# Attention with a routed expert layer on one core: ten head pairs instead of eight have two query tiles turned by DMA, and the first expert weights load five steps later

## The chip, the core and the metric

The kernel runs on one core of a Trainium2 chip. Its engines are PE (TensorE: matmuls and transposes; PEld are its weight loads), DVE (VectorE), ACT (ScalarE), POOL (GpSimd) and SP (SyncE, which here only issues DMAs). The metric is the device time of one execution in microseconds (us), lower is better. A verdict compares the medians of kernels that were timed on the same chip.

## The reference

Attention for 4 batches, 8 heads, 576 positions and 64 features per head, with a bias that a two-layer net computes from the relative position, and behind it an expert layer in which each token goes through one of 8 experts (512 to 1024 to 512). The output is the expert layer's.

```python
scores = scale * np.matmul(q, k.transpose(0, 1, 3, 2))
...
scores = scores + bias.transpose(2, 0, 1)[None, :, :, :]
scores = scores - np.max(scores, axis=-1, keepdims=True)
attn = np.exp(scores)
attn = attn / (np.sum(attn, axis=-1, keepdims=True) + 1e-09)
return np.matmul(attn, v).astype(np.float32)
...
fresh_e = int(np.argmax(logits[b, s]))
if s == 0 or local_gate[b, s] < 0.5:
    e = fresh_e
else:
    e = prev_e if prev_e >= 0 else fresh_e
...
h = np.maximum(x[b, s] @ w1[e], 0.0)
out[b, s] = p[e] * (h @ w2[e])
```

Here x is the attention's output, logits and local_gate are two small products of it, and p is the softmax of the logits.

## The kernel before

**Pairs and units.** Heads are worked in pairs (p, b): p is 0 to 3 (heads 2p and 2p+1), b the batch. The 16 pairs come in the order of the list `pairs`: p = 0 and p = 1 for all four batches, then (2,0), (2,1), (3,0), (3,1), (2,2), (2,3), (3,2), (3,3). From the fifth pair on each pair is nine units: four query tiles of 128 rows with two heads each, and one tile that holds the last 64 rows of both heads. `emit_s` makes a unit's scores: four f16 matmuls into a PSUM tile `sps` (lines 305, 306; 316 for the last tile), of which there are two buffers, then DVE adds the bias and finds the extreme (line 325), then ACT takes the exponential with its row sum (line 330).

**Turning e.** The second product needs the exponentials e with keys on the partitions. There are two ways.

- By TensorE (`emit_t`, `emit_av`): per unit four f32 transposes into PSUM tile `ta` (line 396), an ACT copy to SBUF tile `eT` (lines 400, 402), per query tile one more transpose into `tb` (line 412) with a DVE copy (line 413), then f32 matmuls with v (lines 422, 426).
- By DMA, for pairs in the list `DMP` and there only for the first two query tiles of the order: ACT casts e to an f16 high part (line 336), DVE subtracts it from e for an f16 low part (`emit_lo`, line 346), SP issues one transposing DMA per query tile (line 350), and `av_split` makes three f16 products from high and low parts (lines 363, 369). The high and low parts of v for such a pair are made two pairs ahead by DVE (line 276) and POOL (line 119). Such a pair's output rows are cast on ACT instead of POOL (line 480), and their store to HBM is issued five units later (`LST`).

**Order of the work.** Calls are collected in a list `ev` with a key in units (`at(u + offset, ...)`) and run in the order of the keys. A Tile scheduler then orders each engine's instructions, except for SP between the units S1 and S2, where SP keeps the order in which the calls stand. Every engine works its own instructions in order.

**Routing beside attention.** When batches 0 and 1 are done, `route_first` runs one step per unit: it finds the first two blocks of 128 tokens that share an expert (matmuls into the same `sps` buffers, two scans and many small operations on DVE), then loads block 0's first-layer weights (`load_w(0, 0)`, 2 MB into the tiles `ws`), and some units later splits them into f16 high and bf16 low parts (`split_ops`: ACT cast line 910, DVE or POOL subtraction lines 917, 119). `fetch_first` gathers the tokens of these two blocks and loads block 0's second-layer weights into `wb`. The table `early` places further splits in the last eight units. A load whose expert is that of the block before is conditional (`cond`) and moves nothing then.

**Memory.** The f16 parts of e and v lie in pools (`dmx`) that `open_w` closes; the weight tiles `ws` and `we` are opened in their place. At unit SL the staging tiles of q and k (`stgx`) are closed and a second-layer weight tile is opened.

**After attention** the routing of all tokens runs beside the layers of blocks 0 and 1, and then the other blocks follow.

Of the kernel before, what the change touches and what calls it, by code (L numbers as in the profile page):

```python
# [17 lines left out]
B, H, S, D = 4, 8, 576, 64  # L18
# [31 lines left out]
def build(tc, nc, io):  # L50
# [202 lines left out]
    groups = [(0, b, qt) for g in (QORD[0:2], QORD[2:]) for bb in ((0, 1), (2, 3)) for qt in g for b in bb]  # L253
    pairs = [(p, b) for p in range(NP - 2) for b in range(B)]
# [3 lines left out]
    units = []  # L258
# [2 lines left out]
            units.append((gi, x))  # L261
    e_t, eT_t, hs_t = {}, {}, {}
    e16_t, v16_t, av_t = {}, {}, {}
    DMP = pairs[B:B + 8]
    dmx = ExitStack()
    dbox = {}
    pend, ucur = [], [0]
# [2 lines left out]
    def prefetch(gi):  # L270
        p, b, qt = groups[gi]
        if (p, b) in DMP and qt == QORD[0]:
            if "e" not in dbox:
# [19 lines left out]
    def emit_s(u):  # L293
# [36 lines left out]
        nc.scalar.activation(out=e, in_=e, func=AF.Exp, scale=-1.0, bias=st[:, 0:1], accum_out=sm)  # L330
        if (p, b) in DMP and qt in QORD[0:2]:
            if hh == 0:
# [21 lines left out]
    def av_split(p, b, part=None):  # L354
# [19 lines left out]
            return  # L374
        eT_t.pop((p, b, 0))
        v16_t.pop((p, b))
        xt = xt_t[p, b] = xt_p.tile([128, SP], F32, name="xt")
        if p >= NP - 2:
            nc.vector.memset(xt[:, S:SP], 0.0)
# [2 lines left out]
    def emit_t(u):  # L382
        gi, hh = units[u]
        p, b, qt = groups[gi]
        g = grp(qt)
        if (p, b) in DMP and g == 0:
            return
# [61 lines left out]
    def emit_rows(p, b, u):  # L449
# [29 lines left out]
        on_act = p == 0 or (p == NP - 1 and b >= 2)  # L479
        (nc.scalar.copy if on_act or (p, b) in DMP else cast_pool)(out=hi, in_=xr)  # L480
        (sub_dve if on_act and (p, b) != (NP - 1, B - 2) else sub_pool)(lo, xr, hi)
# [90 lines left out]
    def open_w():  # L572
        dmx.close()
        ws = ctx.enter_context(tc.tile_pool(name="ws0", bufs=1, side="right"))
        for c in range(2):
            stage_t[0].append(ws.tile([128, 2048], F32, name=f"ws0{c}"))
        rbox["w"] = ctx.enter_context(tc.tile_pool(name="we", bufs=1, side="right"))
# [62 lines left out]
    NU = len(units)  # L640
    ex_t = {}

    def emit_out(p, b, gi):
        emit_rows(p, b, gi + 1)
        if (p, b) == DMP[-1]:
            open_w()

    def emit_gates(p, b):
        if p >= NP - 2:
# [106 lines left out]
    def route_first():  # L756
# [78 lines left out]
            in1=tv.unsqueeze(3).to_broadcast([128, NQ, b1, K1]), op=ALU.mult,  # L835
        )
        one_hots(ng, RHA1, RHP1)
        yield
        load_w(0, 0)
        yield  # L840
        ps = s_ps.tile([128, 2, 512], F32, name="sps")
# [3 lines left out]
        nc.vector.tensor_scalar(out=ex, in0=ex, scalar1=-1.0, scalar2=1.0, op0=ALU.mult, op1=ALU.add)  # L845
        nc.vector.tensor_tensor(out=R["tokb"][:, :, 0:b1], in0=ex, in1=tv, op=ALU.mult)
        yield
        for _ in range(3):
            yield
        for f in split_ops(0, 0, on_pool=((1, 1),)):  # L850
            f()
# [228 lines left out]
    for u in range(NU):  # L1080
        gi, hh = units[u]
        p, b, qt = groups[gi]
# [25 lines left out]
    ev.sort(key=lambda e: e[0:2])  # L1108
    ev = [e for e in ev if e[0] < NU]

    S1, S2 = [min(u for u in range(NU) if groups[units[u][0]][0:2] == pairs[i]) for i in (B + 0, B + 9)]
    SL = 1 + min(u for u in range(NU) if groups[units[u][0]][0:2] == pairs[-3])

    def run(a, b):
        for key, _, f in ev:
# [409 lines left out]
```

## Time and profile before

| What | Value |
|---|---|
| median of 3 runs | 581.9 us (580.81 to 582.47) |
| the profiled execution | 579.53 us, of which its span is 577.7 us |
| PE busy | 530.2 us (92%) |
| DVE busy | 468.2 us (81%) |
| ACT busy | 436.6 us (76%) |
| POOL busy | 260.4 us (45%) |
| mean granted TensorE clock | 0.979 of full speed |

The span is the time from the first to the last instruction; 1.83 us of the profiled execution lie around it. Busy shares are means over stages that differ: the bias tables and p = 0 come up to about 130 us, the other pairs up to about 340 us, and then the expert blocks to the end. Matmuls are pipelined and their ends are modelled, so a PE that is shown busy isn't PE at its peak; where a price of PE is wanted, it is better taken from the starts of instructions that follow each other.

### The profile page before, as it was taken

What the parts mean: (1) busy time and instruction counts of PE and PEld (TensorE: products, weight loads), DVE (VectorE), ACT (ScalarE), POOL (GpSimd) and SP (SyncE); (2) the same over time, 40 slices, a digit from 0 to 9 for tenths busy, and PEclk for the clock granted to TensorE, in tenths of its full rate; (3) what the DMA queues carried; (4) which work ended last, traced back from release to release, by engine and by line L of the source; (5) the groups of instructions that cost most, each with busy time, mean ns of one, the idle gap of its engine ahead of it and who ended that gap; (6) DMA issues with size and microseconds to landing.
All of it is one profiled execution on the core that took longest, in us unless ns stands there. A gap on an engine that the chain in (4) does not pass through costs nothing. (4 is left out here: it accounts for less than half of the span.)

```text
span 577.7 us, 14240 instructions
## 1 busy us (share of the span) xinstructions
PE 530.2 (92%) x5302; PEld 359.0 (62%) x5319; DVE 468.2 (81%) x914; ACT 436.6 (76%) x742; POOL 260.4 (45%) x293
## 2 busy tenths in 40 slices
PE   5679999989978999999899999999999999999991
PEld 1124445756755667767586676577686867777851
DVE  6888885688888989797888468779999799898950
ACT  5879877867978887877589865468998787986840
POOL 5200000795299969858547560622433354334111
PEclk9799999999999999999999998799999999999997
DMA  8766546756798799646084012866999947878240
GB/s 278 258 175 186 143 133 194 262 161 154 193 240 226 204 255 247 188 105 190 23 289 117 2 42 71 218 220 218 290 260 293 332 146 191 161 214 225 36 180 30
DMA packets 99613, 106.15 MB, mean 184 GB/s; under 512 B 66893, under 2 KB 76239, under 8 KB 95442
## 3 DMA queue, kind: packets, MB, share of 16 engines
q1 hardware_dynamic: 94752, 89.45, 55.0%
q0 software_dynamic: 4640, 15.43, 9.1%
q8 instruction: 44, 0.72, 0.5%
q10 hardware_dynamic: 146, 0.30, 0.2%
q14 instruction: 31, 0.25, 0.1%
HBM read 128.92 MB, written 20.80 MB: 259 GB/s over the span
## 5 line engine op out<-in xcount | busy, mean ns | idle before, releaser
L330 ACT ACTIVATE e<-e,st 128x576 f32<-128x576 f32 x144 | 111.5, 776 | 16.5 <-DVE st L325 13.1
L325 DVE CUSTOM_DVE_ANT_0 e<-sps,wb 128x576 f32<-128x576 f32 x144 | 107.0, 749 | 18.1 <-PE sps L306 13.3
L917 DVE TENSOR_TENSOR w<-wb,w 128x2048 bf16<-128x2048 f32 (+1 forms) x36 | 72.3, 2050 | 1.9 <-ACT w L910 1.6
L402 ACT COPY eT<-ta 128x512 f32<-128x512 f32 x96 | 55.0, 582 | 21.8 <-PE ta L396 14.6
L305 PE MATMUL sps<-kh,qs 128*128 128x288 f16 x256 | 68.3, 288 | 3.4 <-DVE st L325 2.8
L1014 POOL DMA_INDIRECT out_dram<-y,odx x17 | 30.3, 1781 | 90.2 <-ACT y L1004 58.9
L396 PE MATMUL ta<-c_cpb,e 128*128 128x128 f32 x448 | 70.1, 277 | 0.2
L306 PE MATMUL sps<-kl,qs 128*128 128x288 f16 x256 | 68.0, 286 | 0.0
L910 ACT CAST w<-wb 128x2048 f16<-128x2048 f32 (+1 forms) x40 | 63.8, 1641 | 2.6 <-DMA wb<-in_w_dram 2.6
L988 PE MATMUL yp<-w,hhT 128*128 128x512 f16 (+1 forms) x255 | 64.3, 384 | 1.5 <-ACT w L910 0.5
L211 PE MATMUL sps<-hd,c_cpa 128*32 128x512 f32 (+17 forms) x352 | 49.2, 517 | 15.0 <-DVE hd L197 10.6
L949 PEld LDWEIGHTS <-we 128*128 128x128 f16 (+1 forms) x1056 | 59.9, 98 | 2.4
L949 PE MATMUL sps<-xT,we 128*128 128x128 f16 (+1 forms) x1056 | 61.1, 219 | 0.0
L426 PE MATMUL av<-eT,vt 128*64 128x320 f32 (+1 forms) x384 | 60.8, 424 | 0.0
L396 PEld LDWEIGHTS ta<-c_cpb,e 128*128 128x128 f32 x448 | 52.0, 141 | 10.0 <-issue 2.2
L197 DVE TENSOR_SCALAR hd<-tab,bp 128x448 f32<-128x448 f32 (+17 forms) x130 | 50.1, 445 | 3.6 <-PE sps L211 3.6
L949 PE MATMUL sps<-xT,wb 128*128 128x128 f16 (+3 forms) x1056 | 50.1, 209 | 0.7 <-issue 0.7
L949 PEld LDWEIGHTS <-wb 128*128 128x128 f16 (+1 forms) x1056 | 48.1, 99 | 3.8 <-issue 2.5
L917 DVE TENSOR_TENSOR we<-ws,we 128x2048 bf16<-128x2048 f32 (+1 forms) x25 | 48.9, 1995 | 1.1 <-ACT we L910 1.1
L988 PEld LDWEIGHTS <-hhT 128*128 128x128 f16 x272 | 26.2, 100 | 30.3 <-issue 3.0
L426 PEld LDWEIGHTS av<-eT,vt 128*64 128x64 f32 x384 | 26.2, 136 | 26.6 <-issue 10.4
L910 ACT CAST we<-ws 128x2048 f16<-128x2048 f32 (+1 forms) x26 | 41.2, 1636 | 0.0
(234 smaller groups left out, 1013.2 us busy)
## 6 DMA issues: line engine op xcount, KB each, us to landing
ws<-in_w_dram SPq DMA_DIRECT2D x34, 1024.0 KB
wb<-in_w_dram SPq DMA_DIRECT2D x34, 1024.0 KB
hs<-in_w_dram SPq DMA_DIRECT2D x20, 1024.0 KB
bias_d<-bv SPq DMA_DIRECT2D x36, 295.5 KB
kf<-in_kt_dram SPq DMA_DIRECT2D x24, 288.0 KB
wb<-bias_d SPq DMA_DIRECT2D x16, 288.0 KB
wb<-bias_d SPq DMA_DIRECT2D x16, 256.0 KB
xrow_d<-xo SPq DMA_DIRECT2D x16, 256.0 KB
```

What stands on the lines that cost most here:

```text
L197: nc.vector.tensor_scalar(out=hd[:, 0:n], in0=tab[:, 0:n], scalar1=bp[:, k:k + 1], scalar2=0.0, op0=ALU.add, op1=ALU.max,)
L305: nc.tensor.matmul(out=ps[:, half, 0:288], lhsT=lq, rhs=kh[:, j], start=True, stop=False)
L306: nc.tensor.matmul(out=ps[:, half, 0:288], lhsT=lq, rhs=kl[:, j], start=False, stop=True)
L325: nc.vector.tensor_tensor_reduce(out=e, in0=ps[:, :, 0:288], in1=bsl, scale=-0.125, scalar=1e30, op0=ALU.add, op1=ALU.min, accum_out=st[:, ...
L330: nc.scalar.activation(out=e, in_=e, func=AF.Exp, scale=-1.0, bias=st[:, 0:1], accum_out=sm)
L396: nc.tensor.transpose(out=ta[:, j, :], in_=e[:, o:o + 128], identity=ident)
L402: nc.scalar.copy(out=eTv[:, :, hh, o:o + 128], in_=ta)
L426: nc.tensor.matmul(out=av[64 * x:64 * x + 64, 0:n], lhsT=vt[:, j, 64 * x:64 * x + 64], rhs=eT[:, 2 * j + x, 0:n], start=False, stop=(j == 3),)
L910: nc.scalar.copy(out=wh[c][:, sl], in_=src)
L917: nc.vector.tensor_tensor(out=wl[c][:, sl], in0=src, in1=wh[c][:, sl], op=ALU.subtract)
L949: nc.tensor.matmul(out=hp.rearrange("p a j -> p (a j)")[:, n * f:n * f + n], lhsT=w[f // 4][:, o:o + 128], rhs=x[:, kt], start=(i == 0), s ...
L988: nc.tensor.matmul(out=yp, lhsT=x[:, kt], rhs=w[kt // 4][:, 512 * (kt % 4):512 * (kt % 4) + 512], start=(i == 0), stop=(i == len(terms) - 1),)
```

## The change

`DMP` takes in two more pairs, (2,2) and (2,3), so ten pairs have their first two query tiles turned by DMA. The pools `dmx` are needed longer by that, so `open_w` moves from the output of the last `DMP` pair into `av_split`, behind the last matmul that reads them. `load_w(0, 0)` comes five steps of `route_first` later, and the four splits of these weights four steps later. Block 1's first-layer load, which stands behind them, thereby comes after the first two of block 1's splits (in `early`), which read the tiles that it would fill; it is conditional on an expert other than block 0's. S2 moves by one pair: SP keeps the written order up to the first unit of (3,2) instead of (2,3). SL moves by 12 units.

```diff
@@ -261,7 +261,7 @@
-    DMP = pairs[B:B + 8]
+    DMP = pairs[B:B + 10]
@@ -374,6 +374,8 @@
             return
         eT_t.pop((p, b, 0))
         v16_t.pop((p, b))
+        if (p, b) == DMP[-1]:
+            open_w()
@@ -642,8 +644,6 @@
     def emit_out(p, b, gi):
         emit_rows(p, b, gi + 1)
-        if (p, b) == DMP[-1]:
-            open_w()
@@ -835,7 +835,8 @@
         one_hots(ng, RHA1, RHP1)
-        yield
+        for _ in range(6):
+            yield
         load_w(0, 0)
@@ -845,7 +846,7 @@
         yield
-        for _ in range(3):
+        for _ in range(2):
             yield
         for f in split_ops(0, 0, on_pool=((1, 1),)):
@@ -1108,8 +1109,8 @@
-    S1, S2 = [min(u for u in range(NU) if groups[units[u][0]][0:2] == pairs[i]) for i in (B + 0, B + 9)]
-    SL = 1 + min(u for u in range(NU) if groups[units[u][0]][0:2] == pairs[-3])
+    S1, S2 = [min(u for u in range(NU) if groups[units[u][0]][0:2] == pairs[i]) for i in (B + 0, B + 10)]
+    SL = 13 + min(u for u in range(NU) if groups[units[u][0]][0:2] == pairs[-3])
```

Lines 377 to 645 of the kernel before stand two lines further down in the changed one (413 becomes 415), those behind line 838 one line.

Three places show how instructions move. The first is DVE in the routing steps of pair (2,3), before (full, thr, gp are small tiles of `route_first`, e16_3451 and c16 its one-hot rows, sps the PSUM tile of scores):

```order
L779 TENSOR_REDUCE full_3901<-nbc_3482 16x1
L780 SCALAR_TENSOR_TENSOR gp_3479<-ca_3899,c_cpb_116 16x2
L325 ISA e_3895,st_3923<-sps_3918,wb0_126 128x576
L325 ISA st_3923 128x1
L785 SCALAR_TENSOR_TENSOR thr_3905<-full_3901,ca_3899 16x1
L413 COPY eT_3928<-tb_r_108 128x128
L788 SCALAR_TENSOR_TENSOR e16_3451<-cs_3481,thr_3905,e16_3451 16x576
L800 COPY cb_3955<-sps_3935 16x2
L791 TENSOR_TENSOR c16_3449<-e16_3451,cs_3481 16x576
L325 ISA e_3943,st_3944<-sps_3938,wb0_126 128x576
L325 ISA st_3944 128x1
L801 SCALAR_TENSOR_TENSOR gp_3479<-cb_3955,c_cpb_116 16x2
```

And with the change, where the two low parts of (2,3) (e16_3846 and e16_3886) stand in the middle of the steps:

```order
L779 TENSOR_REDUCE full_3893<-nbc_3482 16x1
L346 TENSOR_TENSOR e16_3846<-e_3842,e16_3846 128x1152
L785 SCALAR_TENSOR_TENSOR thr_3897<-full_3893,ca_3891 16x1
L325 ISA e_3882,st_3934<-sps_3929,wb0_126 128x576
L325 ISA st_3934 128x1
L788 SCALAR_TENSOR_TENSOR e16_3451<-cs_3481,thr_3897,e16_3451 16x576
L800 COPY cb_3954<-sps_3940 16x2
L791 TENSOR_TENSOR c16_3449<-e16_3451,cs_3481 16x576
L325 ISA e_3948,st_3949<-sps_3943,wb0_126 128x576
L325 ISA st_3949 128x1
L346 TENSOR_TENSOR e16_3886<-e_3882,e16_3886 128x1152
L801 SCALAR_TENSOR_TENSOR gp_3479<-cb_3954,c_cpb_116 16x2
```

Between the same two routing operations (lines 779 and 801) two large subtractions have come in, and the copy of line 413 has gone. The second place is SP's queue from pair (2,3)'s loads to the weights, before:

```order
L145 DMA vt_3828<-in_vl_dram 128x640
L490 DMA xrow_d_60<-xo_3775 128x4x128
L493 DMA xrow_d_60<-xo_3775 64x128
L631 DMA xrow_d_60<-pr_3448 128x4x8
L634 DMA xrow_d_60<-pr_3448 64x8
L878 TENSOR_LOAD emap_405
L878 ISA x2
L884 ISA
L884 DMA ws00_3783<-in_w1_dram 128x2048
```

And with the change:

```order
L145 DMA vt_3817<-in_vl_dram 128x640
L350 DMA_TRANSPOSE eT_3889<-e16_3846 128x18x128
L492 DMA xrow_d_60<-xo_3760 128x4x128
L495 DMA xrow_d_60<-xo_3760 64x128
L350 DMA_TRANSPOSE eT_3889<-e16_3886 128x18x128
L879 TENSOR_LOAD emap_405
L879 ISA x2
```

The two transposing DMAs of (2,3) stand between the loads of q, k and v for (3,3) and the read of the expert's number, and the probabilities' store (line 631) has moved ahead of those loads. The third place is ACT behind the last unit of attention, before (w110 and w101 are second-layer weight parts, wb1 holds block 1's first-layer parts, sums the row sums, tmb the gate logits' addends):

```order
L910 CAST w110_4613<-wb0_126 128x1024
L480 CAST xo_4663<-xr_79 128x5x128
L910 CAST w110_4613<-wb0_126 128x1024
L446 ACTIVATE sums_121<-sums_121 128x5x2
L910 CAST w101_4614<-wb0_126 128x1024
L539 COPY tmb_4708<-lg_120 128x45
```

And with the change:

```order
L911 CAST w110_4619<-wb0_126 128x1024
L482 CAST xo_4669<-xr_79 128x5x128
L911 CAST w110_4619<-wb0_126 128x1024
L911 CAST wb1_127<-ws01_4168 128x1024 x2
L448 ACTIVATE sums_121<-sums_121 128x5x2
L911 CAST w101_4620<-wb0_126 128x1024
L541 COPY tmb_4714<-lg_120 128x45
```

Two casts of block 1's weights, which stood earlier, now stand ahead of the last row sums.

## Rows read from the trace of the kernel before

**Rows 1.** Windows: each engine's busy us (instructions), PE clock, DMA share, GB/s.

```profile
237.40:252.60 15.20, 14.62 (x133) 10.71 (x134) 13.20 (x34) 12.92 (x30) 13.00 (x15) 1.00 0.58 161
252.60:269.60 17.00, 16.47 (x149) 12.64 (x148) 12.24 (x48) 13.81 (x34) 8.76 (x12) 1.00 0.53 150
269.60:292.40 22.80, 20.46 (x169) 13.58 (x168) 20.23 (x71) 14.85 (x37) 14.16 (x20) 1.00 0.23 65
292.40:309.70 17.30, 17.30 (x150) 13.11 (x149) 13.87 (x37) 15.78 (x34) 6.83 (x8) 1.00 0.80 277
309.70:328.50 18.80, 18.17 (x140) 12.64 (x139) 11.43 (x35) 16.33 (x34) 13.81 (x21) 1.00 0.14 31
```

**Rows 2.** Timeline of PE: start us, us, instructions; two neighbours, f32 transposes.

```profile
266.00 0.60 PE L396 MATMUL ta<-c_cpb,e 128*128 128x128 f32 x4
266.44 0.27 PE L412 MATMUL tb_r<-c_cpb,e 128*128 128x128 f32 x1
```

**Rows 3.** Timeline of PE: the f32 product, and the split product with what follows it.

```profile
330.18 0.60 PE L422 MATMUL av<-eT,vt 128*128 128x256 f32 x2
...
332.58 0.66 PE L396 MATMUL ta<-c_cpb,e 128*128 128x128 f32 x4
...
254.91 0.49 PE L363 MATMUL av<-eT,v 128*128 128x256 f16 x3
255.33 0.63 PE L369 MATMUL av<-eT,v 128*64 128x256 f16 x8
255.89 0.30 PE L305 MATMUL sps<-kh,qs 128*128 128x288 f16 x1
```

**Rows 4.** One line's instructions, ns min/median/max; then groups: busy us, mean ns.

```profile
L346 DVE TENSOR_TENSOR e<-e,e x16: 1346/1590/2208, 132.3 to 248.1; 128x1152 f16<-128x1152 f32 x16
...
L413 DVE COPY eT<-tb_r 128x128 f32<-128x128 f32 x48 | 13.4, 279 | 7.5 <-PE av L426 3.0 <-issue 2.7 <-PE tb_r L412 1.6
L276 DVE CAST v<-vt 128x640 f16<-128x640 f32 x8 | 6.8, 849 | 4.4 <-DMA vt<-in_vl_dram 4.4
L402 ACT COPY eT<-ta 128x512 f32<-128x512 f32 x96 | 55.0, 582 | 21.8 <-PE ta L396 14.6 <-PE av L426 4.0 <-PE av L434 3.1
L336 ACT CAST e<-e 128x576 f16<-128x576 f32 x32 | 20.7, 668 | 1.1 <-DMA eT<-e 1.0
L910 ACT CAST we<-ws 128x1024 f16<-128x1024 f32 x5 | 5.1, 1052 | 0.0
```

**Rows 5.** Timeline of DVE: one small operation in two stages, and a low part.

```profile
257.15 0.19 DVE L617 TENSOR_TENSOR oh<-oh,mo 128x40 f32<-128x40 f32 x1
273.53 0.70 DVE L617 TENSOR_TENSOR oh<-oh,mo 128x40 f32<-128x40 f32 x1
...
248.05 1.84 DVE L346 TENSOR_TENSOR e<-e,e 128x1152 f16<-128x1152 f32 x1
```

**Rows 6.** Timeline of POOL: first and last of pair (3,3)'s casts.

```profile
270.49 1.41 POOL L122 TENSOR_SCALAR qs<-qf 64x576 f16<-64x576 f32 x2
...
276.25 2.80 POOL L119 TENSOR_TENSOR kl<-kf,kh 128x288 f16<-128x288 f32 x4
```

**Rows 7.** Timeline of SP: a transposing DMA, the weights' loads, and a conditional one.

```profile
250.62 2.08 SPq L350 DMA_TRANSPOSE eT<-e  x1
...
289.46 0.93 SPq L884 DMA_DIRECT2D ws<-in_w_dram  x2
...
297.58 0.76 SPq L884 DMA_DIRECT2D wb<-in_w_dram  x2
...
318.23 0.09 SPq L884 DMA_DIRECT2D wb<-in_w_dram  x1
```

**Rows 8.** Timeline of ACT and of DVE behind attention.

```profile
337.78 0.21 ACT L446 ACTIVATE sums<-sums 128x10 f32<-128x10 f32 x1 [0.95 <-DVE sums L442]
...
338.83 0.25 ACT L539 COPY tmb<-lg 128x45 f32<-128x45 f32 x1
...
339.46 0.29 DVE L544 TENSOR_REDUCE lg<-tmb 128x45 f32<-128x135 f32 x1
```

## The prediction

> **What bounds the kernel now.** I read the windows first, cut where PE begins a pair's last scores: the stages of (3,1), (2,2), (2,3), (3,2) and (3,3), called Z, A, B, C and D here [rows 1]. The reader is to see in them which engine has least room. In A PE is busy 16.47 of 17.00 us and DVE only 12.24: PE sets A's pace. In B, where the routing steps run, PE has 20.46 and DVE 20.23 of 22.80: neither is full, each waits for the other, as scores and routing steps share two PSUM buffers. In C PE is busy throughout, in D 18.17 of 18.80, with ACT next (15.78 and 16.33). Z is a stage whose pair already has its tiles turned by DMA: 15.20 us, PE 14.62, DVE 13.20, so DVE has 2.0 us left in it. The granted clock is 1.00 in all five, the higher of its two levels (2.4 GHz), so no term below is a clock term. The chain of waits ends in the last output DMAs and says nothing about these stages.
>
> **PE's part of the change.** Per new pair 16 transposes into `ta` and two into `tb` go. Four take 0.44 us from start to start [rows 2], so 18 take 2.0 us; those of (2,2) lie in A, those of (2,3) in B. The f32 product of the first two tiles takes 2.40 us (332.58 less 330.18), the split one 0.42 for its first three matmuls and 0.56 for eight of the other 24, so 2.1 in all [rows 3]: a gain of 0.3, in B for (2,2), in C for (2,3). PE's work becomes 14.5 in A, 18.2 in B and 17.0 in C.
>
> **DVE's part.** Per new pair two low parts come and two copies of 0.28 go [rows 4]. A low part took 1.35 to 2.21 us, 1.59 in the median [rows 4], and 1.84 at 248.05 in Z, when POOL worked too [rows 5]. I take 1.75, near Z's, since POOL works for (3,2) in A and for (3,3) in B. That is 3.5 less 0.56, or +2.9 us in A and +2.9 in B: 15.2 and 23.2. In B something comes back: small routing operations of 0.19 us took 0.70 there [rows 5] while POOL cast (3,3)'s q and k from 270.5 to 279.1 [rows 6]. In the new order these casts stand behind the output rows of (3,1) and later loads, so the small operations run free and larger ones meet the casts instead. One such operation shows 0.5; I take 0.8 for all, with 0 and 1.0 as ends, and have 22.4.
>
> **The Trainium skill, SBUF — State Buffer, § Who interferes with whom,** says that a DVE instruction with two SBUF inputs and a POOL instruction that reads SBUF lock each other out for a whole instruction. A low part is such an instruction; by that rule each in B could wait for a whole POOL instruction, which is the longer form of the DVE-bound rival below. The trace agrees in kind (0.70 against 0.19, 1.84 against 1.35).
>
> **Stages.** A is then bounded by DVE: 15.2 with no idle time, 17.2 with Z's 2.0. I take the middle, 16.2: **-0.8** (-1.8 to +0.2). B: 22.4 and half of its 2.57 idle, as PE now has 4 us of room and answers sooner: 23.7, **+0.9**. Its ends are 22.2 without idle time (-0.6) and 23.2 with all of it (+3.0). C is PE's: **-0.3** (-0.6 to 0). In D two more casts of 1.05 [rows 4] come to ACT than stood there before, 18.4 of 18.8: **0** (0 to +0.5).
>
> **Tail.** Two casts of block 1's weights move ahead of the last row sums on ACT, some 2.1 us. ACT had waited 0.95 there, so tmb, ending at 339.08, comes about 1 us later; the reduction that needs it began at 339.46 [rows 8]: **+0.5** (0 to +1.0) on the routing chain, which the expert blocks wait for.
>
> **What costs nothing, and why.** ACT's casts for the high part, 0.67 for a copy of 0.58 [rows 4], add 0.4 in A and in B, where ACT keeps 2 us and more. v's high parts, 0.85 each [rows 4], go into Z and the stage ahead of it, into DVE's 2.0 idle; POOL's share of that finds 2.2 us idle in Z [rows 1]; without this cover up to +0.8. The two hi casts of output rows leave POOL for ACT, in C beside 1.5 us of room that three weight casts leaving C enlarge. Each of four transposing DMAs holds SP about 2.1 us [rows 7]. Queued behind them are row stores, the expert's number and the weights; the loads of (3,2) and (3,3) stand ahead of them. (3,3)'s loads now also stand behind the store of batch 1's probabilities, but its scores are wanted two stages later. The transposes themselves are awaited by the split products: in Z the second was issued at 250.62 and its products began at 254.91 [rows 3, 7], and the new pairs have the same spacing in the order.
>
> **The Trainium skill, VectorE: DVE Perf Modes, § The three transpose paths,** gives 1309 ns for a 128x128 turn by DMA against 390 ns on TensorE. Worked out from the page, an estimate, the 18 blocks of one tile would take 23.6 us, and PE would stand still for most of a stage. The trace differs: 4.3 us from issue to use; the measurement decides, and the sum has no such wait.
>
> The **moved loads** go from 289.46 and 297.58 [rows 7] to where (2,3)'s last split product frees their memory, about 298 in C. The casts that need them stand four units later, so both shift by a like amount; 0, and what it costs otherwise is a rival. Block 1's conditional load now makes SP wait for POOL's parts of the first two splits, but it moves nothing: such an issue took 0.09 us [rows 7]. The gathers of the first two blocks come some units later too and are wanted only behind attention.
>
> **Sum.** -0.8 + 0.9 - 0.3 + 0 + 0.5 = +0.3 us, between -3.0 and +5.5 with all ends together. The profiled execution of 579.53 us (span 577.7 and 1.83 around it) becomes 579.8; it lies 2.4 below the median shown, so the median becomes 581.9 + 0.3 = 582.2. About 0.3%, 1.75 us, is what a measurement of this kernel can tell from no change.
>
> **Rivals.**
>
> *Faster: the new pairs run like Z.* For: Z holds all of this work in 15.2 us, and B's idle time is mutual waiting, which fewer matmuls shorten. Against: A already has the 13 small gate operations of batch 0 on DVE, which Z lacks, so DVE would have to be full at 15.2. Taking the low ends, A -1.8, B -0.6 and C -0.6: 581.9 - 3.0 = 578.9.
>
> *Slower: DVE becomes the bound in B.* Scores wait for line 325 to free one of two PSUM buffers, and that line now queues behind two low parts in the middle of the routing steps. If B keeps its 2.57 us of DVE idle time, which are answers of PE to routing steps, and gets no relief from POOL, it takes 25.8; A 17.2, C 17.0, the tail 0.5: +0.2 + 3.0 - 0.3 + 0.5 = +3.4, or 585.3; with each of B's low parts at the longest seen, 2.21 [rows 4], 586.2. It decides once DVE's work in B passes 23 us. For: no stage of rows 1 has DVE above 0.89 of its time, and the forecast's B needs 22.4 of 23.7, which is 0.95. Against: in those stages PE was as full or fuller.
>
> *Slower: the change doesn't hide its loads.* The first 2 MB took until about 297.6, 8.1 us after their issue [rows 7]. Issued at 298, the first half lands about 302, the whole at 306. If ACT reaches the first cast before that, it stands still with the copies of `ta` behind it, and PE, full in C, stops with it. With 2 to 3 us of that: 584.4. Against: four units are some 8 us.
>
> **Chances.** Forecast (within 1.75 us) 0.45, its own range 580.2 to 583.6; like Z 0.25; DVE-bound 0.22; late loads 0.08. So faster 0.25, same 0.45, slower 0.30. The range reaches past both rivals' times, with about one in ten left out at each end: 578.6 to 585.6.
>
> **What would show it.** Right: the stage of (2,2) about 16 us and that of (2,3) 23 to 24.5, DVE above 0.92 in both, four more rows of line 346 of 1.6 to 1.9 us, PE idle 4 us or more in B, behind line 325. Wrong towards faster: B under 22.5. Wrong towards slower: B above 25 with PE waiting for `st`, ACT waiting for `ws` in C, or PE waiting for `eT` ahead of line 363. The terms of D and the tail are wrong if ACT waits for `ws` at the last two casts of `wb1`.

## The result and the profile after

The changed kernel took **586.56 us** in the median (581.15 to 590.15 over 18 runs) against 580.9 us for the kernel before: a ratio of 1.0081, with a 95% interval of 1.0058 to 1.0104. It is slower by 0.8%, where no change was forecast; the number lies 4.4 us over the forecast and 1.0 us outside the range. The same kernel sent once more gave 1.0048 (1.0012 to 1.0084), and the kernel before against itself 1.0025 (0.9994 to 1.0055). So the loss is real, 3 to 5 us large, and a difference of 0.3% between two kernels tells nothing.

The windows of the changed kernel, cut at the same marks as [rows 1] and with the same columns, show the stages A, B, C and D:

```profile
256.40:271.50 15.10, 14.57 (x133) 10.66 (x134) 13.90 (x47) 13.16 (x32) 8.41 (x8) 1.00 0.70 166
271.50:298.40 26.90, 22.70 (x166) 13.36 (x167) 23.69 (x69) 15.42 (x36) 19.57 (x25) 0.83 0.52 126
298.40:316.00 17.60, 17.60 (x161) 13.39 (x162) 12.79 (x43) 16.23 (x36) 4.74 (x5) 0.96 0.65 248
316.00:332.80 16.80, 16.80 (x132) 11.78 (x131) 12.25 (x34) 15.85 (x33) 10.51 (x14) 1.00 0.33 91
```

A fell from 17.00 to 15.10 us, which is more than forecast. B grew from 22.80 to 26.90, DVE's busy time in it from 20.23 to 23.69 and POOL's from 14.16 to 19.57, and its granted clock fell to 0.83: part of it ran at 1.2 GHz, where all five stages of [rows 1] ran at 2.4. C is 0.3 longer, D 2.0 shorter.

Two more readings are needed. The first is the time ahead of the change: A begins at 256.4 us here and began at 252.6 before, although up to (3,0)'s last scores, at 241.8 and 237.4 us, PE and ACT have the same instructions and DVE and POOL one high and one low part of v more. The second is what follows D: from (3,3)'s last scores to the first matmul of the second expert block's weights (`wb`) it took 17.1 us before and 19.4 now; I call that stretch the tail. The table gives both, and the stages, for each kernel whose trace is used below; all lengths are differences between the starts of PE rows in its timeline.

| kernel | A begins | A | B (clock) | C | D | tail | A to tail | ratio to before (95%) |
|---|---|---|---|---|---|---|---|---|
| before | 252.6 | 17.1 | 22.8 (1.00) | 17.3 | 18.8 | 17.1 | 93.1 | |
| g2 before again | 255.6 | 17.1 | 22.8 (1.00) | 17.3 | 18.8 | 17.1 | 93.1 | 1.0025 (0.9994-1.0055) |
| change | 256.4 | 15.1 | 26.9 (0.83) | 17.6 | 16.9 | 19.4 | 95.9 | 1.0081 (1.0058-1.0104) |
| e4 change again | 251.7 | 15.1 | 27.9 (0.83) | 17.2 | 16.9 | 19.4 | 96.5 | 1.0048 (1.0012-1.0084) |
| e1 nine pairs | 256.9 | 15.1 | 23.8 (1.00) | 17.3 | 18.9 | 17.1 | 92.2 | 0.9981 (0.9951-1.0010) |
| h3 nine again | 253.3 | 15.1 | 25.5 (0.87) | 17.3 | 18.8 | 17.1 | 93.9 | 1.0004 (0.9973-1.0034) |
| e2 only (2,3) | 258.5 | 17.1 | 25.4 (0.85) | 17.8 | 18.1 | 18.9 | 97.2 | 1.0094 (1.0061-1.0127) |
| e3 late loads | 256.5 | 17.1 | 22.9 (1.00) | 18.0 | 19.4 | 18.5 | 95.9 | 1.0045 (1.0016-1.0074) |
| g1 late casts | 256.0 | 17.0 | 22.8 (1.00) | 17.3 | 18.1 | 18.5 | 93.7 | 1.0048 (1.0010-1.0085) |
| f1 filler | 257.4 | 16.8 | 25.4 (0.93) | 17.0 | 17.0 | 19.4 | 95.7 | 1.0055 (1.0020-1.0089) |
| f2 no low part | 256.0 | 15.1 | 21.9 (1.00) | 16.9 | 17.4 | 19.4 | 90.8 | 1.0004 (0.9972-1.0036) |
| f3 casts later | 256.5 | 15.1 | 22.9 (0.93) | 18.4 | 17.9 | 19.4 | 93.8 | 1.0051 (1.0024-1.0077) |
| f4 stores behind | 258.5 | 15.1 | 23.1 (0.93) | 18.7 | 16.9 | 19.4 | 93.2 | 1.0067 (1.0040-1.0095) |
| g4 f3 and f4 | 257.6 | 16.0 | 21.7 (0.92) | 18.6 | 17.4 | 19.4 | 93.2 | 1.0029 (0.9995-1.0063) |
| h1 loads early | 256.6 | 15.1 | 24.5 (0.86) | 17.1 | 16.9 | 19.4 | 92.9 | 1.0020 (0.9983-1.0058) |
| h2 gap filled | 254.6 | 15.1 | 27.8 (0.89) | 17.9 | 17.6 | 19.8 | 98.2 | 1.0137 (1.0086-1.0188) |

The reader is to see two things. A's beginning moves between 251.7 and 258.5 us and is no property of a kernel: the two traces of the change are 4.7 us apart there, those of before 3.0. From A to the tail the two traces of before agree to 0.1 us in every stage, so this is where kernels are compared. There the change is 2.8 and 3.4 us longer, +0.5 and +0.6%; the intervals of its two measurements have 0.6 to 0.8% in common. Z, which holds a second high and low part of v in the change, is shorter there, 14.6 us in both traces against 15.1 in both of before; counted from Z on, the change is 2.2 and 2.9 us longer.

### The profile page after: what moved, and what is told of

Same layout as the page of the kernel before. It is cut to its first block, busy times and chain, and to the rows that moved or that the text cites. A ratio compares the mean times of both kernels' runs of the same rounds, so it can differ in the third digit from the quotient of the medians.

```text
span 583.1 us, 14235 instructions
## 1 busy us (share of the span) xinstructions
PE 532.0 (91%) x5301; PEld 357.5 (61%) x5301; DVE 474.8 (81%) x916; ACT 438.3 (75%) x744; POOL 267.7 (46%) x293
## 5 line engine op out<-in xcount | busy, mean ns | idle before, releaser
L325 DVE CUSTOM_DVE_ANT_0 e<-sps,wb 128x576 f32<-128x576 f32 x144 | 106.8, 748 | 21.7 <-PE sps L306 15.7
L330 ACT ACTIVATE e<-e,st 128x576 f32<-128x576 f32 x144 | 111.5, 775 | 17.1 <-DVE st L325 16.7
L305 PE MATMUL sps<-kh,qs 128*128 128x288 f16 x256 | 70.5, 296 | 2.9 <-DVE st L325 2.2
L306 PE MATMUL sps<-kl,qs 128*128 128x288 f16 x256 | 70.0, 294 | 0.0
L1015 POOL DMA_INDIRECT out_dram<-y,odx x17 | 28.7, 1691 | 85.9 <-ACT y L1005 50.3
L398 PE MATMUL ta<-c_cpb,e 128*128 128x128 f32 x416 | 66.6, 282 | 1.7 <-ACT e L330 0.7
L404 ACT COPY eT<-ta 128x512 f32<-128x512 f32 x88 | 50.4, 580 | 23.4 <-PE ta L398 17.2
L989 PE MATMUL yp<-w,hhT 128*128 128x512 bf16 (+1 forms) x272 | 65.4, 383 | 1.1 <-ACT w L911 1.1
L211 PE MATMUL sps<-hd,c_cpa 128*32 128x512 f32 (+17 forms) x352 | 48.1, 511 | 16.1 <-DVE hd L197 10.6
L398 PEld LDWEIGHTS ta<-c_cpb,e 128*128 128x128 f32 x416 | 49.5, 144 | 11.9 <-ACT e L330 3.2
L428 PE MATMUL av<-eT,vt 128*64 128x320 f32 (+1 forms) x352 | 56.0, 427 | 0.0
L950 PE MATMUL sps<-xT,wb 128*128 128x128 f16 (+3 forms) x1056 | 48.5, 207 | 0.0
L119 POOL TENSOR_TENSOR qs<-qf,qs 64x288 f16<-64x288 f32 x48 | 40.6, 864 | 1.7
## 6 DMA issues: line engine op xcount, KB each, us to landing
wb<-bias_d SPq DMA_DIRECT2D x16, 256.0 KB
xrow_d<-xo SPq DMA_DIRECT2D x16, 256.0 KB
```

The costliest lines, as they stand in the source:

```text
L305: nc.tensor.matmul(out=ps[:, half, 0:288], lhsT=lq, rhs=kh[:, j], start=True, stop=False)
L306: nc.tensor.matmul(out=ps[:, half, 0:288], lhsT=lq, rhs=kl[:, j], start=False, stop=True)
L325: nc.vector.tensor_tensor_reduce(out=e, in0=ps[:, :, 0:288], in1=bsl, scale=-0.125, scalar=1e30, op0=ALU.add, op1=ALU.min, accum_out=st[:, ...
L398: nc.tensor.transpose(out=ta[:, j, :], in_=e[:, o:o + 128], identity=ident)
L404: nc.scalar.copy(out=eTv[:, :, hh, o:o + 128], in_=ta)
L428: nc.tensor.matmul(out=av[64 * x:64 * x + 64, 0:n], lhsT=vt[:, j, 64 * x:64 * x + 64], rhs=eT[:, 2 * j + x, 0:n], start=False, stop=(j == 3),)
```

## Where B's time went

**DVE.** Rows of DVE in the timeline of the changed kernel, one low part of (2,2) in A and both of (2,3) and four short routing operations in B:

```profile
264.80 1.35 DVE L346 TENSOR_TENSOR e<-e,e 128x1152 f16<-128x1152 f32 x1
...
279.55 0.76 DVE L325 CUSTOM_DVE_ANT_0 e<-sps,wb 128x576 f32<-128x576 f32 x1 [1.81 <-PE sps L306]
...
284.29 0.77 DVE L776 TENSOR_SCALAR nbc<-c_cpb,ca 16x9 f32<-16x9 f32 x1
...
285.94 1.33 DVE L346 TENSOR_TENSOR e<-e,e 128x1152 f16<-128x1152 f32 x1
287.20 0.68 DVE L785 SCALAR_TENSOR_TENSOR thr<-full,ca 16x1 f32<-16x1 f32 x1
...
290.73 1.34 DVE L346 TENSOR_TENSOR e<-e,e 128x1152 f16<-128x1152 f32 x1
292.00 0.68 DVE L801 SCALAR_TENSOR_TENSOR gp<-cb,c_cpb 16x2 f16<-16x2 f32 x1
292.61 0.77 DVE L805 TENSOR_SCALAR ecm<-c_cpb,cb 8x2 f32<-8x2 f32 x1
```

A low part took 1.35 us in A and 1.33 in B, and not the 1.75 of the forecast. But lines 785, 801 and 805 took 0.14, 0.14 and 0.21 in the kernel before and take 0.68, 0.68 and 0.77. Thirteen operations that both kernels have in B (line 341 and twelve of 603 to 805) cost 2.2 us more than before in sum, 1.8 of it in lines 776 to 805, where the forecast had 0.8 us less. DVE's account of B is then: low parts +2.7, copies that are gone and work that is now behind the mark -1.4, the thirteen +2.2, which is the 3.5 seen.

What stands beside them is POOL's casts of (3,3), in POOL's timeline (its first two rows are casts of (3,2), in A and B):

```profile
267.51 4.03 POOL L119 TENSOR_TENSOR qs<-qf,qs 64x288 f16<-64x288 f32 x4
...
272.90 2.85 POOL L119 TENSOR_TENSOR kl<-kf,kh 128x288 f16<-128x288 f32 x4
...
282.00 2.24 POOL L122 TENSOR_SCALAR qs<-qf 64x576 f16<-64x576 f32 x2 [4.73 <-PE sps L305]
284.31 4.25 POOL L119 TENSOR_TENSOR qs<-qf,qs 64x288 f16<-64x288 f32 x4
288.65 2.01 POOL L122 TENSOR_SCALAR kh<-kf 128x576 f16<-128x576 f32 x2
290.63 4.10 POOL L119 TENSOR_TENSOR kl<-kf,kh 128x288 f16<-128x288 f32 x4
```

They ran from 282.00 to 294.73 us, through the second half of the routing steps; in the kernel before from 270.49 to 279.05 [rows 6], ahead of that half. They are longer too, 12.7 us instead of 8.6. Single casts show how the two engines hold each other up:

```profile
285.79 2.08 POOL L119 TENSOR_TENSOR qs<-qf,qs 64x288 f16<-64x288 f32 x1
...
290.63 2.04 POOL L119 TENSOR_TENSOR kl<-kf,kh 128x288 f16<-128x288 f32 x1
```

The cast of 285.79 took 2.08 us, where one of this shape took 0.73 at 271.98 in the kernel before: the low part of 285.94 to 287.27 ran beside it. Line 785, right behind the low part, ended at 287.88, with that cast; line 801 ended at 292.68 in the same way, with the cast of 290.63.

Why the casts come late is seen in SP's queue, of the change first:

```profile
270.69 1.92 SPq L350 DMA_TRANSPOSE eT<-e  x1
277.76 0.39 SPq L633 DMA_DIRECT2D xrow_d<-pr  x1
...
278.76 0.58 SPq L141 DMA_DIRECT2D qf<-in_qt_dram  x1
```

and of the kernel before:

```profile
261.88 0.58 SPq L141 DMA_DIRECT2D qf<-in_qt_dram  x1
262.50 7.00 SPq L143 DMA_DIRECT2D kf<-in_kt_dram  x2
...
282.70 0.54 SPq L631 DMA_DIRECT2D xrow_d<-pr  x1
```

Before, (3,3)'s `qf` was issued at 261.88, behind the loads of (3,2) and two row stores, and the store of batch 1's probabilities came 21 us after it. In the change that store and both turned tiles of (2,2) stand ahead, and the load is issued at 278.76, 17 us later. Of these, A's own beginning makes 3.8, and SP's wait for `pr` 5.2 (272.61 to 277.76). **The Trainium skill, SBUF — State Buffer, § Who interferes with whom,** says that DVE's `tensor_scalar` can, for some operands, take the port pair shared with POOL, and that whoever comes second then waits for the other's whole instruction. The trace agrees in kind: line 805, a `tensor_scalar` on 8x2 numbers, took 0.77 us instead of 0.21 with the casts beside it.

**PE.** Rows of PE's timeline at the start of B:

```profile
273.25 0.49 PE L398 MATMUL ta<-c_cpb,e 128*128 128x128 f32 x3
275.35 0.50 PE L363 MATMUL av<-eT,v 128*128 128x256 f16 x3 [1.60 <-DMA eT<-e]
...
277.59 0.42 PE L305 MATMUL sps<-kh,qs 128*128 128x288 f16 x1
...
283.78 0.30 PE L305 MATMUL sps<-kh,qs 128*128 128x288 f16 x1
```

PE stood still for 1.60 us ahead of line 363, for the second turned tile of (2,2), issued at 270.69 and used 4.7 us later; in the second trace of the change (e4, below) it was 0.87 us. DVE then waited 1.81 us for the scores that PE made behind these products (line 325 at 279.55). Right after PE's stand-still the clock fell: the same matmul of line 305 took 0.42 us at 277.59 and 0.30 at 283.78. From about 296 to 300 us it fell again.

So there were three theories. **One**: DVE bounds B, by its low parts and by routing operations that meet POOL's casts. **Two**: PE's idle time and the low clock after it set B. **Three**: the later weights cost the time.

## Experiments: one part of the change alone

**e1: nine pairs**, the first weights where they stood before (S2 and the splits' place too, and SL three units later than before). The edit is shown against the change.

```
-    DMP = pairs[B:B + 10]
+    DMP = pairs[B:B + 9]
...
-        for _ in range(6):
-            yield
+        yield
         load_w(0, 0)
...
```

> Only (2,2) is added (nine pairs); the first weights and the first two splits stand where they stood before. Low parts of (2,2) lie in A, none lies in B. If B's loss comes from the two low parts of (2,3) among the routing steps, A gains 1.9 us, B stays at about 22.8, and the time is 2 us under before, 579. If it comes from PE's wait for the second turned tile of (2,2) (1.60 us ahead of line 363) and the lower clock behind it, that wait stays: B is 25 to 26, and the time is 581 to 583. If it comes from the later loads, the time is 579 and C stays at 17.3.

Measured 579.99 us, 0.9981 (0.9951 to 1.0010). Its B, and B in a second run of it (h3), in the windows of each kernel:

```profile
272.00:295.80 23.80, 20.19 (x179) 13.51 (x178) 21.53 (x72) 15.53 (x39) 17.25 (x25) 1.00 0.43 116
```

```profile
268.40:293.90 25.50, 22.59 (x179) 14.57 (x178) 20.88 (x72) 15.51 (x39) 17.32 (x25) 0.87 0.38 102
```

> Nine pairs with the early weights once more, for the interval and a second trace. If (2,2) alone is a gain of 1 us, 579.5 to 580 again, B 23.8 and no low clock in B; if the first result was chance, 581.

h3 took 580.33 us, 1.0004. A's gain of 2.0 us is there both times and C, D and tail are those of before; B gives 1.0 to 2.7 of it back. So (2,2) alone is worth nothing that can be measured. These two rows say more: the same program had B at 23.8 us with full clock and at 25.5 with a clock of 0.87. So B was 1.7 us longer with the low clock, while DVE was no busier (20.88 against 21.53).

**e2: only (2,3).**

```
+    DMP = pairs[B:B + 8] + pairs[B + 9:B + 10]
```

> Only (2,3) is added (nine pairs), with the change's later loads. Its two low parts, 2.7 us, lie in B; A is as before, 17.0. If DVE's low parts among the routing steps cost the time, B is 25 or more and the time 584 or more. If the wait for the turned tile of (2,2) and the clock behind it cost it, B is 22 to 24 and the time 580 to 582. If the later loads cost it, C is 19 or more.

Measured 586.53 us, 1.0094: the whole loss of the change, without A's gain. B, in the windows:

```profile
275.60:301.00 25.40, 21.86 (x156) 14.45 (x158) 21.58 (x68) 14.60 (x35) 16.41 (x20) 0.85 0.41 108
```

B is 25.4 us with a low clock. Theory one's number came out, but theory two's mark did as well: without (2,2)'s turned tile there still was a low clock in B.

**e3: late loads.** Eight pairs, with only the first weights' load, their casts and the opening of block 1's memory as late as in the change.

```
-        yield
+        for _ in range(6):
+            yield
         load_w(0, 0)
...
-        for _ in range(3):
+        for _ in range(2):
             yield
         for f in split_ops(0, 0, on_pool=((1, 1),)):
...
-    SL = 1 + ...
+    SL = 13 + ...
```

> Eight pairs as before; only the first weights' load, their casts and the opening of the block 1 memory come as late as in the change. If the later loads and the moved casts cost the time, 3 us or more over before, 584 or more, with waits of ACT for ws in C or D. If not, within 1 us of before, and A and B at 17.0 and 22.8.

Measured 584.31 us, 1.0045 (1.0016 to 1.0074). A and B are those of before to 0.1 us; C, D and the tail together are 55.9 us instead of 53.2. So the later weights do cost, 2.6 us by the ratio and 2.7 by the trace. ACT did not wait for `ws`, as theory three had it. PE waited for the routing of batch 2; its wait for `fk` in the waits of e3 around the end of D:

```profile
PE rpa L684 <- DVE fk L618: 1.2, 1, 1.2
```

and in the kernel before:

```profile
PE rpa L684 <- DVE fk L618: 0.2, 1, 0.2
```

The change has the same 1.2. **g1** then left the loads early and moved only the casts.

```
-        for _ in range(3):
+        for _ in range(7):
             yield
         for f in split_ops(0, 0, on_pool=((1, 1),)):
...
-    SL = 1 + ...
+    SL = 13 + ...
```

> Eight pairs; the first weights load when they did before, only ACT's casts of them (line 911) and what follows in that generator come four units later, as in the change. If the 2.6 us of the later loads are the place of the casts (they fall among the last row sums and the routing of batch 2 on ACT), this kernel is 2.5 us over before as well, with PE waiting 1.2 us for fk ahead of line 684. If they are the wait for the weights or the moved loads on SP, it is within 1 us of before.

Measured 582.21 us, 1.0048 (1.0010 to 1.0085). The wait for `fk` is 1.2 us here as well, and the tail 18.5 as in e3. So the casts' place, with SL's, makes the tail longer by 1.4. C and D lost nothing in its trace (A to tail +0.6), while its time is that of e3; whether the loads add something to the casts isn't settled by this.

**e4: the change again.**

> The changed kernel once more, for a second trace. If the 3.8 us that were lost ahead of (3,1), where both kernels have the same instructions, are a matter of the one execution, this trace has (3,1)'s last scores near 238 to 240 and its low-clock stretches in other places, while B again has one. If they belong to the change, the same stretches (122, 170, 224 us) are at 1.2 GHz again.

Measured 584.12 us, 1.0048. Its windows, cut at the same marks:

```profile
251.70:266.80 15.10, 14.57 (x133) 10.66 (x132) 13.90 (x47) 13.16 (x32) 8.20 (x9) 1.00 0.68 178
266.80:294.70 27.90, 22.88 (x164) 14.53 (x163) 23.46 (x68) 15.47 (x36) 19.05 (x25) 0.83 0.44 115
294.70:312.00 17.30, 17.30 (x161) 13.17 (x162) 12.90 (x45) 16.12 (x36) 4.53 (x5) 0.99 0.66 248
312.00:328.80 16.80, 16.80 (x132) 11.78 (x131) 12.25 (x34) 15.85 (x33) 10.51 (x14) 1.00 0.34 95
```

A began at 251.7, earlier than in any other trace of the table, and B has a low clock again, now at 271 to 275 and at 288 to 295 us. **g2: the kernel before again.**

> The kernel before once more, for a second trace. All other traces have 256 us and more up to (2,2)'s last scores, but for one of 251.7 us, that of before 252.6, with the same instructions there. If that is chance, this trace lies anywhere between 251 and 259 us, with low-clock stretches at 122, 170 or 224 us, and (2,2) to (3,3) at 76 us as in the first. If the changed kernels are slower there for a reason, it lies at 252 to 253 again.

Measured 581.56 us. A began at 255.6, behind two stretches of low clock at 166 and 224 us that the first trace does not have. What was lost ahead of the change in its profiled run is chance.

## Experiments: what in B costs

**f2: no low part in B.**

```
-        nc.vector.tensor_tensor(out=e16[:, 1], in0=e, in1=e16[:, 0], op=ALU.subtract)
+        if (p, b) == DMP[-1]:
+            nc.scalar.copy(out=e16[:, 1], in_=e16[:, 0])
+        else:
+            nc.vector.tensor_tensor(out=e16[:, 1], in0=e, in1=e16[:, 0], op=ALU.subtract)
```

> The changed kernel; the low parts of (2,3)'s two turned tiles are not computed, ACT copies the high part in their place (1.0 us each), so DVE has 2.7 us less in B; loads, turns by DMA and PE's work are those of the change. If DVE bounds B, B falls by 2.5 or more, to 24.4 or less, and the time by 2.5. If the low clock sets it, B stays at 26 or more, or moves by no more than its clock does.

This kernel leaves (2,3)'s low parts out, so its output is not the reference's; its expert blocks did the same work, as behind the tail both kernels moved 44.79 MB in as many DVE, ACT and POOL instructions. Measured 580.35 us, 1.0004 (0.9972 to 1.0036): 2.6 to 4.5 us under the change by its two ratios. B, in the windows:

```profile
271.10:293.00 21.90, 18.14 (x160) 11.16 (x160) 19.47 (x66) 16.30 (x37) 16.32 (x24) 1.00 0.64 153
```

B fell by 5.0 us to 21.9, and 4.2 of it is DVE's busy time, of which the two low parts are 2.7. The clock was full, although PE's idle time (3.8 of 21.9 us) has the same share as in the change (4.2 of 26.9). So most of what B lost hangs on DVE's work; the rest may be the clock, which this kernel changed as well. POOL's casts of (3,3) stand here where the change has them (281.69 to 291.07), yet of the three short operations, lines 788, 804 and 808 in this kernel, only one is long:

```profile
284.66 0.14 DVE L788 SCALAR_TENSOR_TENSOR thr<-full,ca 16x1 f32<-16x1 f32 x1
...
285.95 0.68 DVE L804 SCALAR_TENSOR_TENSOR gp<-cb,c_cpb 16x2 f16<-16x2 f32 x1
286.56 0.21 DVE L808 TENSOR_SCALAR ecm<-c_cpb,cb 8x2 f32<-8x2 f32 x1
```

So the casts alone do not make all of these operations long.

**f3: casts of (3,3) later.**

```
-            if qt == QORD[0]:
+            if qt == (QORD[3] if (p, b) == pairs[-3] else QORD[0]):
                 nx = gi // NQ + 2
```

> The changed kernel; the loads of (3,3) and their casts on POOL are issued six units later, so they leave B for C, where POOL was idle; the same instructions otherwise. If DVE bounds B, and the short routing operations of 0.65 to 0.8 us (0.15 to 0.2 alone) are long because POOL casts beside them, DVE's busy time in B falls by 2 us, B to 25 or less, and the time by 2 us. If they are long for another reason, DVE's time and B stay. If the clock sets B, B changes by no more than 1 us.

Measured 583.14 us, 1.0051 (1.0024 to 1.0077). B in the windows, and three rows of DVE's timeline:

```profile
271.60:294.50 22.90, 19.89 (x164) 12.15 (x163) 20.81 (x66) 14.81 (x35) 6.08 (x11) 0.93 0.43 96
```

```profile
286.28 0.14 DVE L785 SCALAR_TENSOR_TENSOR thr<-full,ca 16x1 f32<-16x1 f32 x1
...
290.31 0.14 DVE L801 SCALAR_TENSOR_TENSOR gp<-cb,c_cpb 16x2 f16<-16x2 f32 x1
290.38 0.21 DVE L805 TENSOR_SCALAR ecm<-c_cpb,cb 8x2 f32<-8x2 f32 x1
```

POOL's busy time in B fell from 19.57 to 6.08 and DVE's from 23.69 to 20.81, with the same instructions; lines 785, 801 and 805 are at 0.14, 0.14 and 0.21 again, though both low parts are there. So the low parts alone do not make them long: with f2, it takes both in one stretch. B fell by 4.0 us, but C and D are 1.8 longer together, where the casts now are. Of the 2.1 us left in the trace the time shows less than the comparisons can tell.

**h1: loads of (3,3) early**, ahead of the store of batch 1's probabilities.

```
-            if qt == QORD[0]:
-                nx = gi // NQ + 2
+            if (qt == QORD[0] and (p, b) != pairs[-3]) or (qt == QORD[3] and (p, b) == pairs[-4]):
+                nx = gi // NQ + 2 + (qt == QORD[3])
```

> The changed kernel, with (3,3)'s loads issued on SP ahead of the store of batch 1's probabilities, behind the second turned tile of (2,2), as they stood ahead of that store in the kernel before. If that store's wait on SP is why POOL's casts of (3,3) fall on the second half of the routing steps, the casts begin at about 276 to 278 us instead of 282, the operations of lines 785, 801 and 805 take 0.14 to 0.2 again, B falls by 1.5 to 3 and the time by 1.5 to 2.5. If the order on SP doesn't matter, B stays at 26 or more and the time with the change.

Measured 582.3 us, 1.0020 (0.9983 to 1.0058). POOL's casts, first and last row, and B in the windows:

```profile
277.49 1.43 POOL L122 TENSOR_SCALAR qs<-qf 64x576 f16<-64x576 f32 x2
...
284.24 3.92 POOL L119 TENSOR_TENSOR kl<-kf,kh 128x288 f16<-128x288 f32 x4
```

```profile
271.70:296.20 24.50, 21.50 (x164) 12.71 (x163) 22.10 (x66) 14.80 (x35) 16.49 (x23) 0.86 0.56 137
```

The casts began at 277.49 and ended at 288.16; lines 801 and 805 are short, line 785 still met them (0.69). B is 2.4 us shorter than in the change, C and D are not longer, and A to tail is 92.9. Moving (3,3)'s loads on SP took away, by the medians, more than half of the change's loss; with this interval not more can be said.

**f1: filler.** PE's 32 transposes put back on a constant, at the removed ones' places.

```
         if (p, b) in DMP and g == 0:
+            if (p, b) in DMP[-2:]:
+                ta = ta_ps.tile([128, 4, 128], F32, name="ta")
+                for j in range(4):
+                    nc.tensor.transpose(out=ta[:, j, :], in_=ident, identity=ident)
             return
```

> The changed kernel, with PE's 32 transposes of the two new pairs put back where they stood, on a constant and read by nobody: PE has 1.8 us more work in A and in B, DVE and ACT what they have in the change. If PE's idle time in B and the lower clock behind it cost the time, the clock of B is 1.00 again, B about 24.5, and the time at or under that of the change less 1 us. If DVE bounds B, B stays at 26 or more even at full clock, and the time is that of the change or up to 3 us more (A gives back up to 1.9).

Measured 583.27 us, 1.0055 (1.0020 to 1.0089). A gave 1.7 us back, as it must when PE bounds it again. B is 25.4 us with a clock of 0.93, shorter than in the change with more work on PE. This fits the low clock costing 1 to 2 us in B, but DVE was 0.9 us less busy as well, so it doesn't separate the two.

**h2: the gap filled.** Twelve transposes of a constant ahead of line 363 of the two new pairs, where PE stood still.

```
+        if part == 0 and (p, b) in DMP[-2:]:
+            for n in range(3):
+                ta = ta_ps.tile([128, 4, 128], F32, name="ta")
+                for j in range(4):
+                    nc.tensor.transpose(out=ta[:, j, :], in_=ident, identity=ident)
```

> The changed kernel, with 12 transposes of a constant (some 1.3 us of PE, read by nobody) ahead of line 363 of (2,2) and of (2,3), where PE waits for the second turned tile. DVE, ACT, POOL and the DMAs have what they have in the change. If the low clock in B comes from that stand-still of PE and costs time, B's granted clock is 0.95 or more and the time 1 to 3 us under the change. If DVE sets B, or the low clock has another start, B and the time are those of the change, or up to 1 us more.

Measured 586.69 us, 1.0137. B in the windows:

```profile
269.70:297.50 27.80, 22.90 (x178) 15.68 (x177) 23.84 (x68) 15.51 (x36) 18.73 (x25) 0.89 0.46 120
```

No low clock followed the filled gap; it came at 291 to 298 us instead, and B is 27.8 us with the same DVE time as in the change (23.84 against 23.69). So B's length doesn't hang on the low clock right behind that stand-still. What the late turned tile itself costs this kernel can't say, as its products began 3.6 us into B, against 3.9 in the change. **f4** took that wait away by the order on SP.

```
-            stores.append((ucur[0] + LST, p, b, xo))
+            stores.append((ucur[0] + LST + 2 * ((p, b) in DMP[-4:-2]), p, b, xo))
```

> The changed kernel; the row stores that stand on SP between the two turned tiles of (2,2), and of (2,3), come behind the second, which is then issued about 1.2 us earlier. If PE's 1.6 us wait ahead of line 363 at the start of B starts the loss there, the wait falls to 0.5 or less, no low clock follows it, and B is 25 or less. If DVE bounds B, B stays at 26 or more.

Measured 584.82 us, 1.0067 (1.0040 to 1.0095). B, in the windows:

```profile
273.60:296.70 23.10, 18.93 (x166) 12.76 (x167) 22.06 (x65) 15.05 (x34) 17.35 (x22) 0.93 0.53 120
```

The wait is gone from PE's list of waits, and B in this one trace is 3.8 us shorter than in the change: DVE is 1.6 us less busy and idle 1.0 us instead of 3.2. But the time is that of the change. A part of this lies ahead of A, where Z took 16.1 us in this trace and 14.6 in the change; counted from Z on, f4 is 1.2 us shorter than the change and 1.0 longer than before. Why its time is no lower than the change's stays open.

## Experiments: is there a better version

**g4: ten pairs with f3 and f4**, and **g3: nine pairs with both**.

> Ten pairs with the change's late loads and casts, (3,3)'s loads and casts six units later, and the row stores behind the second turned tile. If the change loses by what lies beside its low parts in B (POOL's casts, the late turned tile and the low clock after it), plus about 2.6 us for the late weights, this is at 581 to 582.5, near before. If its low parts alone cost the time, 584 or more.

> Nine pairs with the first loads where they stood before, (3,3)'s loads and casts six units later, and the row stores behind the second turned tile of (2,2). If A's gain stands by itself, if casts beside the routing steps lengthen them, and if the wait for the turned tile costs 1.2 us, A is 15.1, B 21 to 22, and the time 578, 3 us under before. If only A's gain is real, 579.5 to 580 as with nine pairs alone.

g4 measured 581.55 us, 1.0029 (0.9995 to 1.0063): with POOL's casts out of B and the wait gone, ten pairs come back to the kernel before, and B to 21.7 us. Against f3, from which it differs by the order of the stores alone and whose clock in B is 0.93 to its 0.92, B is 1.2 us shorter with DVE as busy (20.73 against 20.81), but A 0.9 longer. g3 measured 579.68 us, 0.9986 (0.9942 to 1.0030), which misses its 578. **h4: nine pairs with (3,3)'s loads early.**

> Nine pairs with the early weights and (3,3)'s loads ahead of the store of batch 1's probabilities. If casts beside the routing steps are what nine pairs still lose in B, B is 22 to 22.8 instead of 23.8 and the time 578 to 579, 2 us under before. If not, as nine pairs alone.

h4 measured 582.05 us, 1.0024 (0.9988 to 1.0061), which misses its 578 to 579; in its trace the casts of (3,3) began 5.8 us into B, as in e1 (5.7), so its edit moved nothing there. No version beats the kernel before by more than its interval.

## Why the prediction was wrong

**A, -0.8: right in sign, too small.** It gave -2.0 in every trace with (2,2) turned and PE's transposes left out, but for g4 (-1.0). DVE was busy 13.90 us and not 15.2, as the low parts took 1.35 instead of 1.75. POOL's casts of (3,2) ran beside both, but here the cast became the longer one: the first of the four at 267.51 took 1.86 us. In the 1.84 that I had gone by [rows 5] it was the part that was held up: the cast beside its beginning, at 247.95, took 0.73. The stage ran a little below its lower end, as in the rival "like Z".

**B, +0.9: this step failed.** It measured +4.1 and +5.1, 3.2 and 4.2 us over the forecast. In the first trace 1.3 of that is DVE's work (23.69 instead of 22.4) and 1.9 its idle time. In the work the low parts were over-priced (2.7 instead of 3.5); what failed is the relief: "In the new order these casts stand behind the output rows of (3,1) and later loads, so the small operations run free and larger ones meet the casts instead", at -0.8, measured +2.2. I had read the order on POOL and had also seen on SP that (3,3)'s loads now stand behind the store of batch 1's probabilities, and costed that at nothing, since the scores "are wanted two stages later". I had also put all four transposing DMAs behind these loads on SP; (2,2)'s two stand ahead of them. The scores were in time; the casts that the load releases were moved onto the second half of the routing, where (2,3)'s low parts stand. f2, f3 and h1 show it. The other part is idle time: 3.2 us (4.4 in e4) where I had 1.3. Two terms were at nothing in it. One is the turned tile, of which I had "the new pairs have the same spacing in the order" and no wait in the sum: PE waited 1.60 us for it (0.87 in e4), and in f4 and g4, where it is on time, DVE's idle time is 1.0, against 2.1 in f3, which has the wait and a clock like theirs. The other is the clock. "So no term below is a clock term" held for A and fell in B: 0.83 in both traces of the change, and B 1.7 us longer in nine pairs, where the same program ran with and without it.

**C, D and tail, -0.3, 0 and +0.5: right in sum, by two errors.** They measured 53.9 and 53.5 us against 53.2. The later weights cost 2.7 there by themselves (e3), of which the tail's +0.5 and the moved loads' 0 held too little: the tail alone is 2.3 longer. What gives it back is D, 1.9 us shorter: PE has 32 transposes of line 398 in it where it had 40, four of the eight having moved into the tail. At 0.44 us for four [rows 2] that is 0.9 us, and PE's 0.6 us of idle time in D are gone; the rest is not traced. So only 12 of (2,3)'s 16 transposes into `ta` left B, and not all.

**The waits that were to show it.** ACT never waited for `ws`. PE did wait 1.60 us for `eT` ahead of line 363, which the text named as a sign of the slower case. By f4 and g4 it is a part of B's loss in the traces; no time shows it alone.

**The rivals.** What happened is the DVE-bound rival in B: its condition, DVE's work in B past 23 us, was met with 23.69. Its 25.8 us for B fell short by the clock and by the lengthened operations, and its A of 17.2 was 2 us too long; the two errors cancel, so that its 585.3, or 586.2 in the longer form, lies near the 586.56 measured by luck. I gave it 0.22, against a forecast whose own B had DVE at 0.95, which no stage of [rows 1] reached. In the change it reached 0.88, no more than before.

**Not settled:** what the low clock and the late turned tile each cost in B of the change itself (no experiment took one away alone); and why f4, and to a lesser degree f2, f3, g1 and g4, are slower than their traces from A to tail. f2's is 2.3 us shorter than that of before, and its time is the same. g2, the kernel before, stood at 1.0025 in the series of g1 and g4, so a part of it may be the series.

## What to carry to other kernels

When an order on one queue changes, follow each load to the work that it releases, and ask beside which engine's instructions that work now runs, not only whether its result is in time. Where DVE is near full, a long DVE operation with two inputs and a cast on POOL hold each other up, and the shortest DVE operations behind them pay whole waits. And before a loss in a profiled run is explained, take a second trace of the kernel before: stages that differ there can't be read.

## What was not expected of the hardware

DVE operations of 1 to 9 columns cost as much beside POOL's casts (0.68 to 0.77 us) as line 325 over 576 columns (0.74 at 287.81), and POOL pays too: the same four groups of casts took 12.7 us there and 8.6 in the kernel before. A low part beside a cast isn't always the one held up: in the change's first trace the four of (2,2) and (2,3) took 1.33 to 1.36 us, and the casts beside three of them 1.9 to 2.1 instead of 0.7. PE's low clock comes and goes between executions of one program: in nine pairs B had it once and once not. Ahead of A it lasted 3.4 to 20.5 us in the sixteen traces of the table, and A began 6.8 us earlier in one than in another, in the main the later the longer the low clock had lasted.
